# A hand-written order of 1477 steps, reordered behind its first fifth: linear attention followed by a gated long convolution

## The chip, the core and the metric

The kernel runs on one core of one Trainium2 chip. Five engines work beside each other on that core, each with an instruction stream of its own that it executes in order: PE (TensorE, matmuls; its weight loads are listed as PEld), DVE (VectorE), ACT (ScalarE), POOL (GpSimd) and SP (SyncE, which only issues transfers here). Sixteen DMA engines move data. The metric is the device time of one execution in microseconds (us), and the median of several runs is compared.

## The reference, cut to what matters

Two layers follow each other. Eight batches (b = 0 to 7), eight heads, 576 positions, head size 64:

```python
proj = einsum('bhsd,df->bhsf', x, w_phi)                  # x is q, then k; 128 features
proj = proj - max(abs(proj), axis=-1)
phi(x) = concat(exp(proj), exp(-proj))                    # 256 features
kv  = einsum('bhsf,bhsd->bhfd', phi(k), v);  z = sum_s phi(k)
x   = (phi(q) @ kv) / (phi(q) . z + 1e-6)                 # heads side by side: 576 x 512
x1, x2, x3 = split(x @ w_proj)                            # 512 -> 3 * 512
x2  = irfft(rfft(x2) * rfft(filter))                      # along the 576 positions
out = (x1 * x2 * x3) @ w_out
```

The Fourier transforms are matmuls with cosine and sine tables that the kernel makes itself.

## The kernel before, in words

The whole program is a list, `PLAN`, of 1477 words. `run` takes them one after the other; each word names a method of the class `Kernel`, its arguments and, behind an `@`, the first of the eight PSUM banks (0 to 7) in which the step works. The methods issue instructions to their engine at once, so **the order of the words on one engine is the order in which that engine executes**, and nothing reorders it later. Between engines only semaphores hold the order: a step waits until its inputs are there and until the bank or buffer that it writes is free. A word with an engine's name (`Oe,DVE,1,2@7`) says which engine does a step that more than one can do.

Per batch b the words are, in the order of the data:

- `load,n,b` (POOL issues it): q, k or v of a batch from HBM, 576 KB. `trh,n,b,X` (SP): transposes one half by DMA.
- `Pk`, `Qn`, `Pkt`, `Qnt` (PE): projections for the maxima; `maxk`, `maxq` (DVE) reduce them; `mhi`, `mlo`, `trm`, `trme` bring the maxima of q into another layout.
- `ex,k,...` and `ex,q,...` (ACT): the exponentials, of a step of `Pk` or of `Pq`; `exkt`, `exqt` for the remainders. `em,g,b,X` (ACT) is the factor from the maxima and `vs,g,b,X` (POOL or DVE) multiplies v with it, for g = p and m.
- `KV` (PE, 72 matmuls) with its copy `KVe`; `NE`, `NEt` (PE) for numerator and denominator; `rc`, `xn` (DVE) divide.
- `trx`, `trxt` (SP): transpose x by DMA into `xT`, for `X1` and `X3` (PE, 8 matmuls each); `X1t`, `X3t` (16 small matmuls) are the remainders. `X1e` copies x1, `tm` (DVE) multiplies it with x3.
- `f1`, `f2` (POOL or DVE): sums and differences of `xn` that fold the Fourier transform (tiles `SD` and `xf`); `F` (PE) transforms, `Fe` copies to `XF`, `Xl` copies its ends; `X2` (PE) projects in the frequency domain, `Y1` (DVE) multiplies with the filter, `m3` (POOL or DVE) adds; `I` or `J` (PE) goes back, and `Ie`, `Ip`, `Im`, `ym` or `yj` finish y.
- `O,b,c` (PE) is the last product, `Oe,engine,b,c` copies it from PSUM to the tile `o`, and `st,engine,b,c,i` stores one half of it (64 rows).

What the change and the prediction touch besides the order are the rings. `o` has four buffers; they are given out in the order in which `Oe` steps stand in the list, so the copy of a fifth result waits until both halves of the first are stored. `at` and `turn_of` pick the buffer. `vp` and `vm` have three buffers, `kn`, `qn`, `vn` two. SP's queue holds the transposes and the stores in one order: what is behind waits for what is ahead.

The line numbers of the changed file are higher by three than those of the file before from the end of the list on (its text has three more lines), so that L295, the copy on ACT, is L298 there.

Of the kernel before, what the change touches and what calls it, by code (L numbers as in the profile page):

```python
# [69 lines left out]
ym,POOL,0,1 J,0,3@2 maxk,2,2@6 KVe,ACT,1,1@4 NE,1,3@4 ym,POOL,0,2 ex,k,m,2,2@6 yj,0,3@2 NE,1,2@0  # L70
rc,1,3@4 KV,2,0@2 ex,k,p,2,2@6 rc,1,2@0 xn,1,3@4 f1,POOL,1,0,0 xn,1,2@0 trx,1,3 Pqt,1@6 Qn,2,0@4
exqt,m,1@6 f1,POOL,1,1,0 O,0,3@0 maxq,2,0@4 exqt,p,1@6 trx,1,2 O,0,0@1 KVe,ACT,2,0@2 f2,DVE,1,0,1
Oe,ACT,0,3@0 f1,DVE,1,1,1 Qn,2,3@2 trh,q,3,1 Oe,ACT,0,0@1 Qnt,2@4 f2,DVE,1,1,0 f2,POOL,1,1,1
NEt,1@6 maxq,2,3@2 O,0,1@1 trh,k,3,0 f2,POOL,1,0,0 rct,1@6 O,0,2@0 xnt,1,0@6 Oe,ACT,0,1@1 xnt,1,1@6
maxqt,2@4 Pk,2,3@2 trh,k,3,1 Oe,ACT,0,2@0 F,1,2@6 maxk,2,3@2 F,1,3@4 Fe,ACT,1,2@6 F,1,0@0 trh,q,3,0
Fe,ACT,1,3@4 X1,1,3@6 Fe,DVE,1,0@0 ex,k,m,2,3@2 Qn,2,2@4 st,SP,0,1,0 X1e,DVE,1,3@6 em,m,2,1 F,1,1@0
vs,POOL,m,2,1 trxt,1 maxq,2,2@4 X1,1,2@7 Fe,ACT,1,1@0 Qn,3,2@0 st,SP,0,1,1 mhi,2 X2,1,2@4
X1e,ACT,1,2@7 maxq,3,2@0 ex,k,p,2,3@2 load,q,4 X3,1,2@5 Y1,1,2@4 mlo,POOL,2 load,q,5 trm,2@2
X2,1,1@3 trme,ACT,2@2 em,p,2,1 tm,1,2@5 vs,POOL,p,2,1 Pq,2,0@1 Y1,1,1@3 Qn,3,0@4 Pq,2,1@6
ex,q,m,2,0@1 X3,1,3@0 maxq,3,0@4 ex,q,p,2,0@1 load,k,4 X1,1,0@3 ex,q,p,2,1@6 tm,1,3@0 Pq,2,2@4  # L80
ex,q,m,2,1@6 Pkt,3@0 X2,1,3@2 maxkt,3@0 X2,1,0@6 exkt,m,3@0 Y1,1,3@2 exkt,p,3@0 X1,1,1@7
ex,q,m,2,2@4 Y1,1,0@6 NE,2,1@0 X1e,ACT,1,1@7 X3,1,0@2 X1e,ACT,1,0@3 rc,2,1@0 m3,POOL,1,0 xn,2,1@0
ex,q,p,2,2@4 NE,2,0@6 tm,1,0@2 X1t,1@3 rc,2,0@6 Pqt,2@4 xn,2,0@6 X1te,ACT,1@3 Pq,2,3@0 exqt,p,2@4
Xl,DVE,1 Pk,3,1@2 f1,POOL,2,0,1 KV,2,1@6 trh,q,4,1 exqt,m,2@4 maxk,3,1@2 ex,q,p,2,3@0 f1,POOL,2,0,0
X2,1,4@4 st,SP,0,0,0 KVe,ACT,2,1@6 ex,q,m,2,3@0 trx,2,0 NE,2,2@6 m3,POOL,1,1 Y1,1,4@4 X3t,1@5
ex,k,p,3,1@2 rc,2,2@6 NEt,2@0 xn,2,2@6 trx,2,1 X3,1,1@4 ex,k,m,3,1@2 tmt,1@5 rct,2@0 f2,POOL,2,0,0
xnt,2,0@0 NE,2,3@6 trx,2,2 xnt,2,1@0 I,1,0@2 rc,2,3@6 f2,POOL,2,0,1 xn,2,3@6 Ie,1,0@2 I,1,1@0
Im,1,0@2 trx,2,3 Ie,1,1@0 J,1,2@6 tm,1,1@4 f1,POOL,2,1,0 Ip,1,1@0 Im,1,1@0 trxt,2 Pk,3,2@4 Ip,1,0@2
Pk,3,0@0 yj,1,2@6 ex,k,p,3,2@4 ym,POOL,1,0 J,1,3@2 st,SP,0,3,0 maxk,3,0@0 ex,k,m,3,2@4 st,SP,0,3,1
X1,2,0@6 ym,POOL,1,1 st,SP,0,0,1 yj,1,3@2 ex,k,p,3,0@0 X3,2,0@7 trh,k,4,1 maxk,3,2@4 load,v,4  # L90
em,m,3,0 ex,k,m,3,0@0 O,1,0@2 X1e,DVE,2,0@6 trh,q,4,0 em,p,3,0 F,2,0@4 f1,DVE,2,1,1 X1,2,2@6
tm,2,0@7 Fe,ACT,2,0@4 f2,POOL,2,1,0 Qn,3,3@4 Pk,3,3@0 f2,POOL,2,1,1 maxq,3,3@4 O,1,2@7 ex,k,m,3,3@0
X1,2,1@3 vs,POOL,m,3,0 Oe,ACT,1,0@2 Oe,DVE,1,2@7 X1e,ACT,2,2@6 F,2,3@4 maxk,3,3@0 F,2,2@6
st,SP,0,2,1 Fe,ACT,2,3@4 O,1,3@2 X1e,DVE,2,1@3 st,SP,1,0,0 ex,k,p,3,3@0 vs,POOL,p,3,0 Fe,DVE,2,2@6
F,2,1@4 yt,ACT,1 Qn,3,1@0 Fe,ACT,2,1@4 Qnt,3@6 X3,2,2@3 maxq,3,1@0 Oe,ACT,1,3@2 em,p,3,1 O,1,4@4
st,SP,1,3,0 vs,POOL,p,3,1 maxqt,3@6 st,SP,1,2,0 X2,2,2@2 tm,2,2@3 mhi,3 Xl,ACT,2 st,SP,0,2,0
mlo,DVE,3 em,m,3,1 st,SP,1,0,1 Qnt,4@6 Qn,4,0@0 X2,2,0@3 load,k,5 trh,k,4,0 maxqt,4@6 Y1,2,2@2
vs,POOL,m,3,1 X3,2,1@5 Oe,ACT,1,4@4 st,SP,1,2,1 O,1,1@6 Y1,2,0@3 st,SP,1,3,1 trm,3@4 X2,2,3@2
Oe,ACT,1,1@6 maxq,4,0@0 trme,ACT,3@4 X1t,2@3 Pq,3,1@6 tm,2,1@5 X1te,ACT,2@3 KV,3,0@0 Y1,2,3@2
ex,q,m,3,1@6 Pq,3,2@4 ex,q,p,3,1@6 KVe,DVE,3,0@0 m3,POOL,2,1 Pq,3,0@2 X2,2,1@0 ex,q,m,3,0@2  # L100
NE,3,1@6 trh,k,5,0 ex,q,p,3,0@2 Y1,2,1@0 X1,2,3@1 ex,q,p,3,2@4 NE,3,0@2 rc,3,1@6 m3,POOL,2,0
xn,3,1@6 X3,2,3@0 ex,q,m,3,2@4 rc,3,0@2 trx,3,1 xn,3,0@2 Qn,4,2@6 X1e,ACT,2,3@1 Pq,3,3@4 maxq,4,2@6
KV,3,1@2 f1,POOL,3,0,0 st,SP,1,1,1 ex,q,p,3,3@4 st,SP,1,4,0 tm,2,3@0 Pkt,4@6 ex,q,m,3,3@4
f1,POOL,3,0,1 trx,3,0 X2,2,4@1 maxkt,4@6 KVe,ACT,3,1@2 Pqt,3@4 f2,POOL,3,0,1 Y1,2,4@1 exkt,m,4@6
trh,k,5,1 NE,3,3@2 exkt,p,4@6 NE,3,2@0 rc,3,3@2 exqt,p,3@4 xn,3,3@2 I,2,1@6 exqt,m,3@4 rc,3,2@0
Ie,2,1@6 trx,3,3 xn,3,2@0 Pk,4,1@2 X3t,2@4 ex,k,p,4,1@2 Ip,2,1@6 f1,POOL,3,1,1 I,2,2@0 tmt,2@4
trx,3,2 Im,2,1@6 Ie,2,2@0 I,2,0@4 ex,k,m,4,1@2 Im,2,2@0 ym,POOL,2,1 Ip,2,2@0 Pk,4,0@6 trh,q,5,1
Ie,2,0@4 J,2,3@0 maxk,4,1@2 ex,k,p,4,0@6 ym,POOL,2,2 ex,k,m,4,0@6 trh,q,5,0 Ip,2,0@4 X1,3,2@2
Im,2,0@4 yj,2,3@0 ym,POOL,2,0 X1,3,0@3 X1e,ACT,3,2@2 st,SP,1,4,1 maxk,4,0@6 Pk,4,3@0 f2,POOL,3,0,0
Qn,4,1@4 O,2,1@2 maxk,4,3@0 em,p,4,0 X1e,ACT,3,0@3 f1,POOL,3,1,0 O,2,0@6 maxq,4,1@4 ex,k,m,4,3@0  # L110
O,2,3@3 f2,POOL,3,1,1 ex,k,p,4,3@0 Oe,DVE,2,0@6 NEt,3@4 Oe,DVE,2,1@2 load,k,6 st,SP,2,0,1
Oe,ACT,2,3@3 Pk,4,2@6 Qn,4,3@0 rct,3@4 em,m,4,0 ex,k,p,4,2@6 X1,3,1@2 xnt,3,0@4 f2,POOL,3,1,0
xnt,3,1@4 maxq,4,3@0 F,3,0@4 trxt,3 ex,k,m,4,2@6 vs,POOL,p,4,0 X3,3,0@3 Fe,ACT,3,0@4 maxk,4,2@6
st,SP,2,3,0 F,3,2@0 mhi,4 X1e,ACT,3,1@2 F,3,3@4 st,SP,1,1,0 Fe,ACT,3,2@0 vs,DVE,m,4,0 F,3,1@6
mlo,POOL,4 Fe,ACT,3,3@4 Qn,5,2@0 em,p,4,1 X1,3,3@2 Fe,ACT,3,1@6 maxq,5,2@0 Xl,ACT,3 X2,3,2@6
X1e,ACT,3,3@2 tm,3,0@3 em,m,4,1 trm,4@0 X2,3,3@1 vs,POOL,m,4,1 trme,ACT,4@0 Y1,3,2@6 Pq,4,1@2
Qn,5,3@4 Y1,3,3@1 trh,k,6,0 Pq,4,0@6 X3,3,1@0 ex,q,p,4,0@6 maxq,5,3@4 m3,POOL,3,1 st,SP,2,0,0
X2,3,0@1 ex,q,m,4,0@6 st,SP,2,1,1 tm,3,1@0 X2,3,1@4 ex,q,p,4,1@2 Y1,3,0@1 load,q,7 KV,4,0@6
ex,q,m,4,1@2 Y1,3,1@4 vs,POOL,p,4,1 Pq,4,2@0 KVe,ACT,4,0@6 Pq,4,3@2 ex,q,m,4,2@0 NE,4,0@6 X3,3,3@4
ex,q,p,4,3@2 rc,4,0@6 load,v,6 xn,4,0@6 O,2,2@5 ex,q,p,4,2@0 m3,POOL,3,0 tm,3,3@4 trx,4,0 NE,4,1@6  # L120
ex,q,m,4,3@2 KV,4,1@0 rc,4,1@6 xn,4,1@6 Oe,ACT,2,2@5 f1,DVE,4,0,0 Qn,5,0@2 trx,4,1 f1,POOL,4,0,1
Pk,5,0@6 KVe,ACT,4,1@0 maxq,5,0@2 X2,3,4@5 ex,k,m,5,0@6 NE,4,2@0 f2,POOL,4,0,0 ex,k,p,5,0@6
Y1,3,4@5 NE,4,3@2 X3,3,2@4 rc,4,3@2 xn,4,3@2 X1t,3@5 rc,4,2@0 trx,4,3 I,3,1@2 xn,4,2@0 X1te,ACT,3@5
# [991 lines left out]
```

## Time and profile before

| what | value |
|---|---|
| median of three runs | 310.7 us (308.33 to 312.73) |
| profiled execution, from its first to its last instruction | 311.6 us |
| PE busy | 281.0 us, 90% |
| DVE busy | 268.6 us, 86% |
| ACT busy | 216.3 us, 69% |
| POOL busy | 203.8 us, 65% |
| moved by DMA | 40.20 MB, 129 GB/s in the mean |
| granted PE clock, mean | 0.974 |

The profiled execution tells no time of its own beside its span; the span is 0.9 us above the median of the three runs and inside their range. A row of the timeline gives the start, the time taken, the engine, the line, the operation with output and inputs, and in brackets how long the engine had been idle before and what ended that. The list of waits gives who waited for whom: us in total, number of times, longest. A row for DMA issues ends with the median from issue to landing. The prediction quotes the rows that it uses.

### The profile page before, as it was taken

How to read it: one execution, taken by the hardware profiler on the slowest of the kernel's cores; microseconds unless marked ns; L12 is line 12 of the kernel's file. 1: busy time of each engine (PE TensorE's matmuls, PEld its weight loads, DVE VectorE, ACT ScalarE, POOL GpSimd, SP SyncE). 2: the span in 40 equal slices, each digit the busy share in tenths (PEclk: the TensorE clock that was granted, in tenths of full speed). 3: DMA queues.
4: the chain of work that ended last, by engine and by line, in shares of the span. 5: the costliest groups of instructions: out<-in, count | busy, mean ns of one | idle time of the engine just before them, and what ended most of it. 6: DMA issues, size and time to landing. Idle time of an engine off the chain costs nothing.

```text
span 311.6 us, 10240 instructions
## 1 busy us (share of the span) xinstructions
PE 281.0 (90%) x4331; PEld 205.3 (66%) x4360; DVE 268.6 (86%) x447; ACT 216.3 (69%) x345; POOL 203.8 (65%) x163
## 2 busy tenths in 40 slices
...
GB/s 162 235 203 159 136 202 193 105 190 133 91 164 204 94 110 170 116 160 107 114 198 82 131 160 153 172 175 160 84 117 4 56 93 69 19 110 21 1 115 192
DMA packets 72735, 40.20 MB, mean 129 GB/s; under 512 B 53040, under 2 KB 67504, under 8 KB 72688
## 3 DMA queue, kind: packets, MB, share of 16 engines
...
q10 hardware_dynamic: 400, 0.66, 0.8%
q8 instruction: 34, 0.56, 0.8%
...
HBM read 33.75 MB, written 9.44 MB: 139 GB/s over the span
## 4 chain that ended last, share of the span: by engine, by line
PE 70%; DVE 12%; DMA 7%; ACT 5%; issue 3%; SPq 1%; POOL 0%; DVEq 0%; POOLq 0%
PE ps L919 16%; PE ps L897 10%; PE ps L1049 8%; PE ps L764 5%; PE ps L972 4%; PE ps L778 4%; DMA xT<-xn 4%; DMA out_dram<-o 3%; PE ps L1028 3%; PE ps L858 3%; PE ps L862 3%; PE ps L928 2%; DVE mq L707 2%; PE ps L665 2%; PE ps L638 2%
## 5 line engine op out<-in xcount | busy, mean ns | idle before, releaser
L919 PE MATMUL ps<-xT,wproj 128*128 128x256 bf16 x512 | 65.8, 275 | 4.3 <-DVE x1s L960 2.3
L919 PEld LDWEIGHTS <-wproj 128*128 128x128 bf16 x512 | 48.6, 98 | 14.5 <-issue 5.1
L707 DVE TENSOR_REDUCE mk<-ps 128x8 f32<-128x1024 f32 (+1 forms) x40 | 44.0, 1110 | 5.9 <-ACT HTo L295 2.2
L707 DVE TENSOR_REDUCE mq<-ps 128x8 f32<-128x1024 f32 (+1 forms) x40 | 44.0, 1110 | 5.5 <-PE ps L638 4.5
L749 POOL TENSOR_TENSOR vm<-vn,vm 128x1152 bf16<-128x1152 bf16 x14 | 30.4, 2178 | 18.2 <-ACT vm L743 18.2
L749 POOL TENSOR_TENSOR vp<-vn,vp 128x1152 bf16<-128x1152 bf16 x16 | 34.8, 2180 | 10.5 <-ACT vp L743 10.3
L911 POOL TENSOR_TENSOR T<-T,T 128x1024 bf16<-128x1024 bf16 x12 | 25.5, 2124 | 21.9 <-DVE T L907 21.8
L693 ACT ACTIVATE Ekp<-ps 128x1024 bf16<-128x1024 f32 x32 | 32.8, 1030 | 6.6 <-DVE mk L707 3.3
L1038 POOL TENSOR_TENSOR yT<-cv,x1s 128x576 bf16<-128x576 f32 x19 | 24.3, 1289 | 18.3 <-DVE x1s L964 12.8
L852 POOL TENSOR_TENSOR xf<-SD 128x512 bf16<-128x512 bf16 x27 | 31.2, 1170 | 6.7 <-DVE SD L846 5.3
L693 ACT ACTIVATE Ekm<-ps 128x1024 bf16<-128x1024 f32 x32 | 32.8, 1033 | 3.6 <-DVE mk L707 2.7
L693 ACT ACTIVATE Eqm<-ps 128x1024 bf16<-128x1024 f32 x32 | 32.9, 1034 | 3.1 <-PE ps L671 2.9
L1049 PE MATMUL ps<-wout,yT 128*128 128x512 bf16 x133 | 34.3, 385 | 0.7 <-issue 0.2
L693 ACT ACTIVATE Eqp<-ps 128x1024 bf16<-128x1024 f32 x32 | 32.5, 1031 | 3.4 <-PE ps L671 3.3
L846 POOL TENSOR_TENSOR SD<-xn 128x512 bf16<-128x512 bf16 x23 | 26.5, 1160 | 12.6 <-DVE xn L797 12.6
L897 PE MATMUL ps<-wproj,XF 128*128 128x512 bf16 x117 | 30.3, 380 | 0.7 <-issue 0.2
L295 ACT CAST x1s<-ps 128x512 bf16<-128x512 f32 (+1 forms) x30 | 16.0, 548 | 13.1 <-PE ps L928 8.4
L797 DVE TENSOR_TENSOR xn<-ps,r 128x512 bf16<-128x512 f32 x32 | 22.0, 689 | 1.1
L1049 PEld LDWEIGHTS <-yT 128*128 128x128 bf16 x144 | 13.4, 99 | 14.1 <-issue 0.6
L990 ACT COPY es<-ps 128x288 f32<-128x288 f32 x21 | 8.5, 404 | 20.3 <-PE ps L972 19.8
L960 DVE TENSOR_TENSOR x1s<-ps,x1s 128x512 bf16<-128x512 f32 x32 | 21.7, 683 | 0.6 <-ACT x1s L295 0.4
L778 PE MATMUL ps<-KVs,Eqp 128*128 128x65 bf16 x256 | 19.6, 192 | 2.2 <-DVE mq L707 0.6
...
## 6 DMA issues: line engine op xcount, KB each, us to landing
out_dram<-o SPq DMA_DIRECT2D x67, 128.0 KB, 2.9
vn<-in_v_dram POOLq DMA_DIRECT2D x8, 576.0 KB, 7.5
kn<-in_k_dram POOLq DMA_DIRECT2D x7, 576.0 KB, 9.7
qn<-in_q_dram POOLq DMA_DIRECT2D x7, 576.0 KB, 6.6
...
fl<-in_moe_filter_fft_dram SPq DMA_DIRECT2D x8, 128.0 KB, 5.8
out_dram<-o ACTq DMA_DIRECT2D x5, 128.0 KB, 2.8
...
```

What stands on the lines that cost most here:

```text
L693: self.nc.scalar.activation(e, p, AF.Exp, bias=0.0, scale=1.0 if g == "p" else -1.0)
L707: self.nc.vector.tensor_reduce(out=out, in_=src, axis=AX.X, op=ALU.max, apply_absolute_value=True)
L749: self.eng(eng).tensor_tensor(out=t[:, :, :, 0:64], in0=self.at("vn", b)[:, 2 * X:2 * X + 2], in1=t[:, :, :, 64:65].to_broadcast([128, 2, ...
L778: self.mm(self.pb(u, 65 * a, 65 * a + 65), E, KVs[:, u, v, s, :], start=(s == 0), stop=(s == 1))
L797: self.nc.vector.tensor_tensor(out=o, in0=n[:, :, :, 0:64], in1=self.at("r", 4 * b + v).to_broadcast([128, 2, 4, 64]), op=ALU.mult)
L846: self.eng(eng).tensor_tensor(out=o[:, :, 2 * i:2 * i + 2, :], in0=x[:, :, 0:2, :], in1=x[:, :, 2:4, :], op=ALU.subtract if i else ALU.add)
L852: self.eng(eng).tensor_tensor(out=o[:, :, 2 * i:2 * i + 2, :], in0=x[:, :, 0:4:2, :], in1=x[:, :, 1:4:2, :], op=ALU.subtract if i else ALU ...
L897: self.mm(self.pb(0), l, w[:, kt, 512:1024], start=(kt == 0), stop=(kt == 3))
L911: self.eng(eng).tensor_tensor(out=Y, in0=Y, in1=self.at(f"T{2 * e + 1}", b), op=ALU.add)
L919: self.mm(o[:, d], w[:, kt, f0 + 128 * m:f0 + 128 * m + 128], y[:, 1, ::-1, ::-1] if d else y[:, 0], start=(kt == 0), stop=(kt == 3))
L1038: self.eng(eng).tensor_tensor(out=self.at("yT", b)[:, m, 0:SEQ], in0=self.turn_of("cv", (b, m)).rearrange("p x h t -> p (x h t)"), in1=sel ...
L1049: self.mm(self.pb(0), y[:, kt, 128 * c:128 * c + 128], w[:, kt, :], start=(kt == 0), stop=(kt == 3))
```

## The change

The list keeps its first 307 words (21 per cent). Behind these the same 1170 steps stand in another order, with three kinds of difference. Steps move by up to 77 places. In 63 steps that more than one engine can do, the engine is another: for example six `X1e`, five `f1`, four `Oe` and three `Fe` go from DVE to the other engine that can do them, and five `X1e`, four `f1`, four `f2`, four `ym`, three `KVe` and three `Xl` come to DVE. And 239 steps work in another PSUM bank. The order on SP (transposes and stores) is the same word for word, and so is the order of the loads among themselves; where a load stands among POOL's other work is not. No method is changed.

A piece of the list, the words in which the two first differ (`em,p,2,0`, the factor for v, now stands ahead of `Pq,1,2`):

```diff
-m3,POOL,0,0 exkt,p,2@2 Qn,2,1@0 X1e,ACT,0,1@5 tm,0,2@7 Pq,1,0@2 Pq,1,2@4 maxq,2,1@0 ex,q,m,1,0@2
+m3,POOL,0,0 exkt,p,2@2 Qn,2,1@0 X1e,ACT,0,1@5 tm,0,2@7 Pq,1,0@2 em,p,2,0 Pq,1,2@4 maxq,2,1@0
```

Three places follow, all around the end of batch 1 and the middle of batch 2 and 3 (about 112 to 131 us in the trace of before).

**DVE, copies between the steps of batch 2.** Before (`o_1123` is the second buffer of the ring `o`, written here by `Oe,DVE,1,2`; `mk_86` and `mq_88` are maxima of batch 3; `XF_138` is `Fe`):

```order
L960 TENSOR_TENSOR x1s_140<-ps,x1s_140 128x2x8x32
L707 TENSOR_REDUCE mq_88<-ps 128x2x4
L297 COPY o_1123<-ps 128x512
L707 TENSOR_REDUCE mk_86<-ps 128x2x4
L297 CAST x1s_140<-ps 128x2x8x32
L297 CAST XF_138<-ps 128x576
L707 TENSOR_REDUCE mq_88<-ps 128x2x4
```

The same place in the changed kernel:

```order
L963 TENSOR_TENSOR x1s_140<-ps,x1s_140 128x2x8x32
L710 TENSOR_REDUCE mq_88<-ps 128x2x4
L710 TENSOR_REDUCE mk_86<-ps 128x2x4
L300 COPY yT_1120<-yT_1121 128x4x64
L710 TENSOR_REDUCE mq_88<-ps 128x2x2
L710 TENSOR_REDUCE mq_88<-ps 128x2x4
```

The copy to `o`, and the two casts that stood behind it, have left DVE; they are on ACT now.

**ACT, the same stretch.** Before (`vp0_104` is `em,p,3,0`, `Ekm3` and `Ekp3` the exponentials of `Pk,3,3`, `o0_1122` `Oe,1,0`, `o2_1124` `Oe,1,3`):

```order
L743 ACTIVATE vp0_104<-mk1_86 128x18
L295 CAST XF0_138<-ps_61 128x576
L693 ACTIVATE Ekm3_110<-ps_61 128x1024
L295 COPY o0_1122<-ps_61 128x512
L295 CAST x1s0_140<-ps_61 128x2x8x32
L295 CAST XF0_138<-ps_61 128x576
L693 ACTIVATE Ekp3_96<-ps_61 128x1024
L295 COPY yT0_1120<-yT1_1121 128x4x64
L295 CAST XF0_138<-ps_61 128x576
L295 COPY o2_1124<-ps_61 128x512
```

In the changed kernel, where `vp1_105` is `em,p,3,0` and `o1_1123` is `Oe,1,3`:

```order
L696 ACTIVATE Ekp3_96<-ps_61 128x1024
L746 ACTIVATE vm0_118<-mk1_86 128x18
L696 ACTIVATE Ekm3_110<-ps_61 128x1024
L298 CAST x1s0_140<-ps_61 128x2x8x32
L298 CAST XF0_138<-ps_61 128x576
L746 ACTIVATE vp0_104<-mk1_86 128x18
L298 CAST XF0_138<-ps_61 128x576
L746 ACTIVATE vp1_105<-mk1_86 128x18
L298 CAST XF0_138<-ps_61 128x576
L298 COPY o1_1123<-ps_61 128x512
L730 CAST mh1_90<-mq1_88 128x2x18
L298 COPY o2_1124<-ps_61 128x512
```

Both copies to `o` stand behind all casts of `F` here, and the factor for `vs,POOL,p,3,0` has moved from ahead of the first cast to between the second and the third.

**POOL, the loads and the products with v.** Before (`kn_78` is `load,k,5`; `vm_118`, `vp_104`, `vp_105` and `vm_119` are `vs` of m,3,0, p,3,0, p,3,1 and m,3,1):

```order
L590 DMA vn_79<-in_v_dram 128x4x576
L852 TENSOR_TENSOR xf_137<-SD_136 128x2x256 x2
L749 TENSOR_TENSOR vm_118<-vn_80,vm_118 128x18x64
L749 TENSOR_TENSOR vp_104<-vn_80,vp_104 128x18x64
L749 TENSOR_TENSOR vp_105<-vn_80,vp_105 128x18x64
L590 DMA kn_78<-in_k_dram 128x4x576
L749 TENSOR_TENSOR vm_119<-vn_80,vm_119 128x18x64
```

In the changed kernel, where `vp_105` is p,3,0 and `vp_104` p,3,1:

```order
L855 TENSOR_TENSOR xf_137<-SD_136 128x2x256
L593 DMA vn_79<-in_v_dram 128x4x576
L752 TENSOR_TENSOR vm_118<-vn_80,vm_118 128x18x64
L752 TENSOR_TENSOR vp_105<-vn_80,vp_105 128x18x64
L593 DMA kn_78<-in_k_dram 128x4x576
L752 TENSOR_TENSOR vm_119<-vn_80,vm_119 128x18x64
L752 TENSOR_TENSOR vp_104<-vn_80,vp_104 128x18x64
```

The load of k for batch 5 has one product with v less ahead of it.

More of the change, by code (lines that the diff above doesn't have):

```diff
@@ L70 @@
[L70 to L123, printed above, removed]
@@ new lines @@
+ex,q,m,2,0@1 X3,1,3@0 X1,1,0@3 ex,q,m,2,1@6 ex,q,p,2,1@6 st,SP,0,1,1 maxq,3,0@4 Pq,2,2@4 tm,1,3@0
+Pkt,3@0 maxkt,3@0 X2,1,3@2 X2,1,0@6 X1,1,1@7 Y1,1,3@2 Y1,1,0@6 exkt,p,3@0 exkt,m,3@0 NE,2,1@0
+X1e,ACT,1,0@3 X3,1,0@2 ex,q,m,2,2@4 X1t,1@3 rc,2,1@0 load,q,4 ex,q,p,2,2@4 X1e,DVE,1,1@7 xn,2,1@0
+tm,1,0@2 NE,2,0@6 Pq,2,3@0 vs,POOL,m,2,1 load,q,5 vs,POOL,p,2,1 rc,2,0@6 Pqt,2@4 X1te,ACT,1@3
+exqt,p,2@4 xn,2,0@6 load,k,4 exqt,m,2@4 Pk,3,1@2 ex,q,m,2,3@0 KV,2,1@6 maxk,3,1@2 ex,q,p,2,3@0
+X2,1,4@5 trh,q,4,1 ex,k,m,3,1@2 KVe,DVE,2,1@6 f1,DVE,2,0,0 m3,POOL,1,1 NE,2,2@6 NEt,2@0
```

219 lines of the change are left out of this document (135 added, 84 removed).

## The prediction

> **What bounds the kernel now.** I read the busy shares first, then busy time by stretches, PE's list of waits, and the timelines of the four engines around the longest wait.
>
> ```profile
> span 311.6 us, 10240 instructions
> PE 281.0 (90%) x4331; PEld 205.3 (66%) x4360; DVE 268.6 (86%) x447; ACT 216.3 (69%) x345; POOL 203.8 (65%) x163
> 65.00:300.00 235.00, 225.80 (x3587) 170.16 (x3610) 207.41 (x321) 163.49 (x261) 157.72 (x113) 0.99 0.70 115
> 118.50:132.32 13.82, 11.16 (x95) 6.67 (x96) 10.26 (x13) 5.53 (x12) 7.84 (x5) 0.88 0.76 139
> ```
>
> The lower two rows are stretches: their length, busy time and count of PE, PEld, DVE, ACT and POOL, then the granted clock of PE, the DMA share and GB/s. PE is the bound. The kept words reach to about 65 us, and what follows 300 us is the end of the last batch. Between them PE is busy for 225.80 of 235.00 us: 9.2 us of idle time is all that an order of the same matmuls can win there, apart from the clock. DVE is busy for 207.41 and idle for 27.6. The list of PE's waits behind 60 us says where the 9.2 lie (total, count, longest):
>
> ```profile
> PE ps L858 <- DVE o L297: 2.4, 1, 2.4
> PE ps L928 <- issue: 1.6, 1, 1.6
> PE ps L919 <- DMA xT<-xn: 1.1, 1, 1.1
> PE ps L778 <- DVE mq L707: 0.6, 1, 0.6
> PE ps L778 <- DVE xn L797: 0.5, 1, 0.5
> ```
>
> These five make 6.2; the rest are pieces of 0.5 and less. I go through the five, then through what is added.
>
> **Term 1, the wait of 2.4 us for `o`.** Before, PE's `F,2,2` and DVE's copy `Oe,DVE,1,2`, the chain of waits, the loads and products on POOL, and the median landing times of stores, first from 222 to 232 us, where no load is in flight, then from 127.9 to 138.4:
>
> ```profile
> 121.20 0.28 PE L858 MATMUL ps<-Dt,xnt 128*128 128x288 bf16 x1 [2.38 <-DVE o L297]
> 120.46 0.69 DVE L297 COPY o<-ps 128x512 f32<-128x512 f32 x1 [2.99 <-DMA out_dram<-o]
> 121.06 1.21 DVE L707 TENSOR_REDUCE mk<-ps 128x8 f32<-128x1024 f32 x1
> 113.32 7.04 DMA out_dram<-o
> 112.66 0.80 POOL L590 DMA_DIRECT2D vn<-in_v_dram  x1
> 122.31 1.02 ACT L693 ACTIVATE Ekp<-ps 128x1024 bf16<-128x1024 f32 x1 [2.94 <-DVE mk L707]
> 125.85 2.15 POOL L749 TENSOR_TENSOR vp<-vn,vp 128x1152 bf16<-128x1152 bf16 x1 [4.57 <-ACT vp L743]
> 127.94 0.80 POOL L590 DMA_DIRECT2D kn<-in_k_dram  x1
> out_dram<-o SPq DMA_DIRECT2D x7, 128.0 KB, 2.4
> kn<-in_k_dram POOLq DMA_DIRECT2D x1, 576.0 KB, 6.8
> out_dram<-o SPq DMA_DIRECT2D x3, 128.0 KB, 6.3
> ```
>
> A store alone lands after 2.4 us. The store `st,SP,0,0,1` was issued at 113.32, 0.66 us behind `load,v,4` (112.66), and took 7.04, about as long as the load itself. DVE stood 2.99 us until that store had freed its buffer. Behind the copy were queued the maxima of k (121.06) and the cast of `F,2,2`, and PE's bank with them.
>
> After the change no copy to `o` is on DVE here. The buffer goes to `Oe,ACT,1,3`, behind the third cast, and by then the store has landed: this wait goes. It was also dear behind its end, since the granted clock from 118.50 to 132.32 is 0.88 against 0.99 in the large stretch: 11.16 x (1 - 0.88/0.99) = 1.2 us of slower matmuls. So 2.4 + 1.2 = 3.6 is at stake.
>
> What is late next? Follow the new order by durations from the rows. Without the stall, the maxima of k end at about 118.7 (DVE's work before the stall ended at 120.46 - 2.99 = 117.47, and the reduce takes 1.21). The exponential behind them and the casts of `x1` and of `F,2,2` on ACT take 1.02 and twice about 0.6 (the copy of 0.59 quoted below has their shape or nearly), one after the other, and `em,p,3,0`, formerly ahead of all casts, ends at about 121.1. Then `vs,POOL,p,3,0` (2.15, as the product at 125.85) ends at 123.3, and `load,k,5`, which has one product less ahead of it, is issued at 123.3 instead of 127.94. On ACT the last cast, `Oe,1,3` and `Oe,1,2` follow until 123.5. SP's queue holds a store of each of the two, and only then `st,SP,0,2,0`, which was issued at 126.76, ahead of the load, and is now issued at about 124.1: 0.8 us behind the load. That is the position of the 7.04 us store. If it holds as that one, it lands with the load at 123.3 + 6.8 = 130.1. `Oe,ACT,1,4` needs that buffer, as it did before, and reads bank 6, which the new order gives to `Pq,3,1` next:
>
> ```profile
> 129.20 0.59 ACT L295 COPY o<-ps 128x512 f32<-128x512 f32 x1 [1.34 <-issue]
> 129.10 1.04 PE L919 MATMUL ps<-xT,wproj 128*128 128x256 bf16 x8
> 129.97 1.03 PE L1049 MATMUL ps<-wout,yT 128*128 128x512 bf16 x4
> 131.76 0.63 PE L928 MATMUL ps<-xTt,wproj 128*128 128x64 bf16 x16
> 132.32 0.28 PE L665 MATMUL ps<-qT,wphi 64*128 64x256 bf16 x2
> ```
>
> Then `Oe,1,4` ends at 130.7 and `Pq,3,1` starts there, instead of at 132.32. But the new order puts `X3,2,1` (0.87 from start to start) and `X1t,2` (0.56) behind it, so 130.89 would be even: the gain is **0.2**. If the store lands alone, at 126.5, PE doesn't meet it and the gain is **3.6**. I take 0.2, since the one store issued at such a distance behind a load took 7.04, and the three from 127.9 on 6.3.
>
> The Trainium skill ("DMA: Bandwidth & Descriptors", Queues, rings and completion order) says that each DMA engine goes round the queues that have work and changes over after a packet, so that a store would not wait for a load of another queue to finish. By it the store would land early and this term would be the 3.6; the trace disagrees with it in the 7.04 us row, and I keep it as a rival.
>
> **Term 2, 1.1 us before `X1,3,2`.**
>
> ```profile
> 149.33 1.25 PE L919 MATMUL ps<-xT,wproj 128*128 128x256 bf16 x10 [1.08 <-DMA xT<-xn]
> 145.49 2.54 SPq L816 DMA_TRANSPOSE xT<-xn  x2
> xT<-xn SPq DMA_TRANSPOSE x2, 2.5
> ```
>
> The transposes are issued behind `xn` and behind SP's earlier work. `Qn,4,1` (8 small matmuls, 0.3 us) moves ahead of the step as filler, and everything before it shifts by the gain of term 1, consumer and producer alike. Bounds: 0 and 1.08; I take **0.5**.
>
> **Term 3, a gap inside a step.** PE stops amid `X1t,3`, between matmuls with the same inputs and the same bank:
>
> ```profile
> 176.46 0.34 PE L928 MATMUL ps<-xTt,wproj 128*128 128x64 bf16 x6
> 178.38 0.47 PE L928 MATMUL ps<-xTt,wproj 128*128 128x64 bf16 x10 [1.58 <-issue]
> q8 instruction: 34, 0.56, 0.8%
> ```
>
> No datum is missing there, and the page lists a queue that brings instructions; I read the gap as a late fetch while loads fill the engines. In a new order the same place in the stream falls in another step, with other transfers beside it: it can vanish (1.58), stay, or be worse. I take half, **0.8**.
>
> The Trainium skill ("Runtime: NRT & Kernel Launch", Instruction fetch mechanics) says that an engine's stream is refilled in blocks of 256 instructions by a queue of its own and that the cost of a boundary is mostly hidden. By it the gap would be no fetch and go whole with the order that made it, 0.8 more; the 1.58 us between two alike matmuls speaks against "hidden".
>
> **Term 4, DVE beside POOL.** `NE` steps wait for DVE twice, 0.6 and 0.5. In both places a fold on DVE runs beside one on POOL:
>
> ```profile
> 114.24 0.41 DVE L846 TENSOR_TENSOR SD<-xn 128x512 bf16<-128x512 bf16 x1
> 172.41 1.48 DVE L846 TENSOR_TENSOR SD<-xn 128x512 bf16<-128x512 bf16 x1
> 208.28 1.41 DVE L846 TENSOR_TENSOR SD<-xn 128x512 bf16<-128x512 bf16 x1
> 208.25 1.16 POOL L846 TENSOR_TENSOR SD<-xn 128x512 bf16<-128x512 bf16 x1 [0.51 <-DVE xn L797]
> ```
>
> Alone it takes 0.41, beside POOL's 1.41. At 208 us the new order has neither fold between the divisions of batch 5: I book the 0.5 whole. At 172 us the fold is gone too, but an `Oe` and an `m3` have come to DVE ahead of the same maxima: 0 to 0.6, I take 0.3. Together **0.8**.
>
> **Term 5, what is added.** DVE gets four `f2` and three `KVe` more than it had before, and gives away copies of similar size:
>
> ```profile
> L852 DVE TENSOR_TENSOR xf<-SD 128x512 bf16<-128x512 bf16 x5 | 4.3, 854 | 0.1
> L297 DVE CAST KVs<-ps 128x520 bf16<-128x520 f32 x6 | 4.2, 694 | 0.7 <-PE ps L764 0.7
> ```
>
> If every one stood on the path, 4 x 0.854 + 3 x 0.694 = 5.5 us; below nothing it can hardly go, as the copies given away are counted in terms 1 and 4. DVE's 27.6 idle us in the stretch cover it, and if that cover is gone at a place, `NE` waits for the copy. New short waits of a kind not seen before must still be expected among 1170 moved steps: **0.5 lost**, one such copy. The 239 bank changes add no instruction; where a bank is freed later, it is a piece of this term.
>
> **The sum**, against the profiled execution's 311.6, which is 0.9 above the median: -0.2 - 0.5 - 0.8 - 0.8 + 0.5 = -1.8, so 309.8 in such a profile and **308.9** for the median of 310.7.
>
> **The rivals.**
>
> *The store lands alone* (A). The 0.8 us behind the load is only 0.14 more than the distance of the one quoted store, and my 124.1 and 123.3 are each a chain of six durations. If the store is issued ahead of the load, or is served between its packets, term 1 is -3.6: 308.9 - 3.4 = **305.5**. Against it: the 7.04 and the 6.3.
>
> *Nearly all idle time goes* (B): all of the 9.2 is won, 310.7 - 9.2 = **301.5**. For it: the steps that wait in the list all have other neighbours now. Against it: the load moved up in term 1.
>
> *`load,k,6` holds back a transpose* (C, slower). Before, POOL waits for `yj` and issues this load late:
>
> ```profile
> 148.63 1.27 POOL L1038 TENSOR_TENSOR yT<-cv,x1s 128x576 bf16<-128x576 f32 x1 [0.31 <-DVE cv L993]
> 153.29 0.80 POOL L590 DMA_DIRECT2D kn<-in_k_dram  x1
> kT<-kn SPq DMA_TRANSPOSE x2, 6.1
> ```
>
> Now it stands directly behind the `ym` of 148.63, ahead of two `f2` and an `f1`, so some 3 to 4 us earlier. The transposes for `X1,3,2` are issued from 145.49 to 148.03. If the load's issue falls ahead of the second by 0.6 us or more, that transpose takes 6.1 instead of 2.5 and PE stands 3.6 us longer: with nothing won in term 2, 308.9 + 0.5 + 3.6 = **313.0**, and up to 315 with a lowered clock behind it. By before's times the `ym` comes two microseconds too late for that; a transpose as much later decides.
>
> *Nothing is won* (D): the gaps come back at other places, as in term 1, in all terms: **310.7**.
>
> **How the numbers follow.** Forecast 0.42, A 0.26, B 0.07, C 0.12, D 0.13. A measurement of this kernel tells about 2% (6.2 us) from no change. Faster, below 304.5: B whole, nearly half of A (305.5, with the open 1.1 of terms 2 and 4 and 0.8 of term 3 below it), and 0.02 of the forecast: 0.21. Slower, above 316.9: C with a second transpose held, and an added copy on the path in several places: 0.09. The range takes in the forecast, A, D and C's own value, leaving out B and the tail of C: 302 to 314. The forecast's own range, by its terms' bounds, is 306 to 312.
>
> **What would show it.** Term 1: PE's first row of waits is gone, and a copy to `o` on ACT at about 126 to 130 us has waited for the store (forecast) or not (A); the store lands about 6 or 2.4 us after its issue. Term 2: the row `X1` behind `xT` below 1.1. Term 3: no gap "issue" over 1 us inside a step. Term 4: folds on DVE of about 0.4. Rival C: transposes of `xT` with 6 us in the stretch behind 145 us. PE's busy time in the stretch should stay at 226, with less idle. The prediction is wrong if a wait of over 2 us stands at a place that I haven't named.

## The result: slower by 4.6 per cent

The changed kernel took 324.34 us in the median (323.87 to 328.97), the kernel before 309.62 us beside it (308.33 to 312.73). The ratio is 1.0457, with a 95% interval of 1.0367 to 1.0548. Forecast were 308.9 us and a range of 302 to 314. Ratios and their intervals here and below leave out runs over 1.5 per cent above the fastest of their kernel (here the one of 328.97), so that they can differ from the ratio of two medians.

Page and list of waits (PE, from 60 us on) of the changed kernel, and PE, PEld, DVE, ACT and POOL in the stretch from 65 to 300 us:

```profile
span 322.1 us, 10234 instructions
PE 281.1 (87%) x4331; PEld 205.4 (64%) x4360; DVE 279.4 (87%) x452; ACT 216.5 (67%) x345; POOL 201.2 (62%) x158
65.00:300.00 235.00, 216.47 (x3504) 163.47 (x3527) 207.14 (x307) 159.23 (x253) 152.64 (x107) 0.99 0.65 112
PE ps L668 <- ACT o L298: 5.9, 1, 5.9
PE ps L922 <- DVE T L910: 2.4, 1, 2.4
PE ps L861 <- DVE xnt L812: 1.4, 1, 1.4
PE ps L975 <- DVE x1s L963: 1.3, 1, 1.3
PE ps L975 <- DVE xn L800: 0.9, 2, 0.4
```

PE's work is the same, 281.1 us against 281.0. In the stretch it was busy for 216.47 us, 9.3 less than the 225.80 before, so it waited that much longer. All five first waits of the kernel before are gone from the list, and new ones have come: one of 5.9 us for a copy to `o` on ACT, and a row of waits for DVE, whose busy time has grown by 10.8 us (279.4 against 268.6).

Where along the program the time was lost can be read by adding up PE's steps in the order of each list, each at its kind's usual time from start to start, and asking when the two profiles reach the same sum:

```
time in the changed kernel, step     later than before by
 80.8  Pk,2,3                         0.5
121.7  O,1,2                         -3.4   (before's wait of 2.4 has gone)
133.6  Pq,3,1                         2.7   (the wait of 5.9)
138.2  X2,2,1                         4.7   (slow matmuls behind it)
154.3  Pk,4,3                         4.0
161.6  F,3,0                          5.5   (wait of 1.4)
177.1  X3,3,3                         8.1   (wait of 2.4)
186.5  I,3,2                          7.3
224.9  F,5,0                          9.8   (waits of 1.3 and 0.8)
the end                              10.5
```

**The first loss, at the place of the prediction's term 1.** In order: POOL, the chain of waits, the DMA issues between 122.9 and 124.9 us, ACT and PE, and the stretch from 126.0 to 139.1.

```profile
123.09 0.80 POOL L593 DMA_DIRECT2D kn<-in_k_dram  x1
124.21 8.55 DMA out_dram<-o
kn<-in_k_dram POOLq DMA_DIRECT2D x1, 576.0 KB, 9.7
out_dram<-o SPq DMA_DIRECT2D x4, 128.0 KB, 7.2
132.92 1.07 ACT L298 COPY o<-ps 128x512 f32<-128x512 f32 x2 [8.10 <-DMA out_dram<-o]
133.56 0.40 PE L668 MATMUL ps<-qT,wphi 64*128 64x256 bf16 x2 [5.91 <-ACT o L298]
126.00:139.10 13.10, 7.14 (x120) 5.33 (x120) 3.56 (x4) 3.80 (x5) 4.79 (x3) 0.74 0.80 140
```

`load,k,5` was issued at 123.09 and `st,SP,0,2,0` at 124.21, 1.1 us behind it. The store took 8.55 us; the load itself, with the stores and a transpose beside it, took 9.7. ACT stood 8.10 us for the buffer and PE 5.91. The granted clock in the stretch around that wait is 0.74 against 0.99: 7.14 x (1 - 0.74/0.99) = 1.8 us of slower matmuls besides. (The mean hides what the clock does: within that stretch it is 0.50 from 131.4 to 138.0 us.)

**The other losses, on DVE.** Three steps on DVE that read and write SBUF alone, and what POOL did at those times:

```profile
158.76 2.37 DVE L855 TENSOR_TENSOR xf<-SD 128x512 bf16<-128x512 bf16 x1
172.53 3.37 DVE L300 COPY XL<-XF 128x512 bf16<-128x512 bf16 x1
219.38 3.19 DVE L849 TENSOR_TENSOR SD<-xn 128x512 bf16<-128x512 bf16 x1
...
158.49 2.36 POOL L752 TENSOR_TENSOR vp<-vn,vp 128x1152 bf16<-128x1152 bf16 x1
172.05 0.80 POOL L593 DMA_DIRECT2D qn<-in_q_dram  x1
172.84 0.75 POOL L593 DMA_DIRECT2D vn<-in_v_dram  x1
173.60 2.14 POOL L914 TENSOR_TENSOR T<-T,T 128x1024 bf16<-128x1024 bf16 x1
```

The first is `f2,DVE,3,1,1`, the second `Xl,DVE,3`, the third `f1,DVE,5,1,1`; before, ACT did the second and POOL the two others. Each ends 0.2 to 0.3 us behind a piece of POOL's work: 161.13 beside 160.85, 175.90 beside 175.74, and the third 222.57 beside 222.27 (there POOL had a load issue from 219.18, then two folds of 1.17 and 1.15). The copy waits through the end of one load issue, a second one and a product in a row. Groups of DVE by form, before and then after:

```profile
L297 DVE COPY XL<-XF 128x512 bf16<-128x512 bf16 x3 | 0.8, 282 | 0.0
...
L300 DVE COPY XL<-XF 128x512 bf16<-128x512 bf16 x4 | 6.2, 1558 | 0.2 <-ACT XF L298 0.2
L855 DVE TENSOR_TENSOR xf<-SD 128x512 bf16<-128x512 bf16 x8 | 8.2, 1037 | 0.1
```

The same copy takes 282 ns in the mean before and 1558 after.

### The profile page after: what moved, and what is told of

Same layout as the page of the kernel before. It is cut to its first block, busy times and chain, and to the rows that moved or that the text cites. A ratio compares the mean times of both kernels' runs of the same rounds, so it can differ in the third digit from the quotient of the medians.

```text
span 322.1 us, 10234 instructions
## 1 busy us (share of the span) xinstructions
PE 281.1 (87%) x4331; PEld 205.4 (64%) x4360; DVE 279.4 (87%) x452; ACT 216.5 (67%) x345; POOL 201.2 (62%) x158
## 4 chain that ended last, share of the span: by engine, by line
PE 57%; DVE 26%; DMA 5%; ACT 5%; issue 5%; ACTq 1%; POOL 0%; SPq 0%; DVEq 0%; POOLq 0%
PE ps L922 13%; PE ps L1052 7%; PE ps L900 7%; PE ps L767 4%; DVE mq L710 4%; DVE mk L710 4%; PE ps L975 3%; PE ps L781 3%; DVE T L910 3%; DMA xT<-xn 3%; PE ps L1031 3%; DMA out_dram<-o 3%; PE ps L861 2%; PE ps L865 2%; DVE cv L996 2%
## 5 line engine op out<-in xcount | busy, mean ns | idle before, releaser
L849 POOL TENSOR_TENSOR SD<-xn 128x512 bf16<-128x512 bf16 x24 | 28.1, 1182 | 35.2 <-DVE xn L800 35.1
L914 POOL TENSOR_TENSOR T<-T,T 128x1024 bf16<-128x1024 bf16 x13 | 27.5, 2122 | 15.0 <-DVE T L910 14.8
L1041 POOL TENSOR_TENSOR yT<-cv,x1s 128x576 bf16<-128x576 f32 x17 | 22.1, 1309 | 13.2 <-DVE cv L996 12.9
L855 POOL TENSOR_TENSOR xf<-SD 128x512 bf16<-128x512 bf16 x24 | 27.4, 1153 | 3.9 <-DVE SD L849 2.0
L298 ACT COPY o<-ps 128x512 f32<-128x512 f32 x21 | 12.2, 592 | 21.3 <-DMA out_dram<-o 11.3
L298 ACT CAST XF<-ps 128x576 bf16<-128x576 f32 x27 | 16.8, 648 | 11.4 <-PE ps L865 11.2
L298 ACT CAST x1s<-ps 128x512 bf16<-128x512 f32 (+1 forms) x30 | 16.7, 556 | 11.4 <-PE ps L922 4.7
L668 PE MATMUL ps<-qT,wphi 64*128 64x256 bf16 x128 | 16.6, 284 | 6.6 <-ACT o L298 5.9
```

What stands on the lines that cost most here:

```text
L298: self.nc.scalar.copy(dst, src)
L849: self.eng(eng).tensor_tensor(out=o[:, :, 2 * i:2 * i + 2, :], in0=x[:, :, 0:2, :], in1=x[:, :, 2:4, :], op=ALU.subtract if i else ALU.add)
L855: self.eng(eng).tensor_tensor(out=o[:, :, 2 * i:2 * i + 2, :], in0=x[:, :, 0:4:2, :], in1=x[:, :, 1:4:2, :], op=ALU.subtract if i else ALU ...
L914: self.eng(eng).tensor_tensor(out=Y, in0=Y, in1=self.at(f"T{2 * e + 1}", b), op=ALU.add)
L1041: self.eng(eng).tensor_tensor(out=self.at("yT", b)[:, m, 0:SEQ], in0=self.turn_of("cv", (b, m)).rearrange("p x h t -> p (x h t)"), in1=sel ...
```

## The experiments

The runs below were made in groups, and in these the kernel before has medians of 308.7 to 313.5 us. So each ratio is against the runs of before in the same group, and where one profile answers the question, PE's row for 65 to 300 us stands beside it.

### The held stores: four runs

Two of the edits change the place of the stores on SP:

```diff
 st,SP,0,2,1 st,SP,1,0,0
+st,SP,0,2,0 st,SP,1,0,1
 st,SP,1,3,0 st,SP,1,2,0
-st,SP,0,2,0 st,SP,1,0,1
 trh,k,4,0
```

> The changed kernel with the stores st,SP,0,2,0 and st,SP,1,0,1 moved ahead on SP, directly behind st,SP,1,0,0; nothing else. Their data lie ready since about 116 us, so they are issued at about 121.6 and 122.2 instead of 124.21 and 124.85, ahead of load,k,5 (123.1). Theory 'held stores': both land after 2.3 to 2.5 us, the copy to o on ACT no longer waits 8.1 us, PE's wait of 5.9 us before Pq,3,1 goes and with it about 2.0 us of matmuls at a lowered clock: 324.3 - 7.9 = 316.4 us (315 to 318). Rival 'the new order itself is late' (the copy or the bank comes late for another reason): the wait stays or moves to the next step of PE, 322 us or more.

Measured: 316.15 us (315.31 to 317.40), 1.034 of before (1.025 to 1.043): 8.2 below the changed kernel. There is no wait for `o` left. ACT copies as soon as the product is there, and PE goes on at 126.14:

```profile
125.38 0.59 ACT L298 COPY o<-ps 128x512 f32<-128x512 f32 x1 [2.01 <-PE ps L1052]
126.14 0.28 PE L668 MATMUL ps<-qT,wphi 64*128 64x256 bf16 x2
65.00:300.00 235.00, 223.93 (x3534) 167.01 (x3553) 210.81 (x318) 160.34 (x255) 153.53 (x107) 0.99 0.65 113
```

So the wait belongs to the place of the stores. Two things were not as expected. The stores were issued earlier still, at 117.04 and 117.68, and took 6.45 and 6.04 us, not 2.3 to 2.5: `load,v,4` (issued at 111.90) and two transposes were in flight there. They landed at 123.5 and 123.7, just in time. And the wait of 2.4 us before `X3,3,3` is gone too, though nothing was changed on DVE: `Xl,DVE,3` now begins 0.20 us into POOL's first load issue instead of 0.48, and is through in its own time, ahead of the same row of POOL's work.

```profile
163.01 0.28 DVE L300 COPY XL<-XF 128x512 bf16<-128x512 bf16 x1
162.81 0.80 POOL L593 DMA_DIRECT2D qn<-in_q_dram  x1
```

In its place stands a gap of 2.2 us ("issue", L931), of which more below. By this profile the two words are worth 7.5 of the 9.3 us of PE's work that the change lost in the stretch; by the ratios, whose kernel before ran shorter in this group, they take the loss from 4.6 to 3.4 per cent.

With only one store moved (the first of the two `+` words):

> As the run before, but only st,SP,0,2,0 is moved ahead; st,SP,1,0,1 stays and is issued behind load,k,5. Theory 'held stores': Oe,ACT,1,4 is free and Pq,3,1 starts at about 127.5 instead of 133.56, but the next copy, Oe,ACT,1,1, needs the buffer of st,SP,1,0,1, which still lands with the load at about 133; PE then waits at Pq,3,2 (bank 4), for about 4 us, and the time falls by 1 to 3 us only (321 to 323). Rival 'one store is the cause': as with both, 316.4.

Measured: 319.11 us in one run, between the two theories' times. The wait moved to the next copy and the next product, as the first theory has it, but it was shorter than expected, 2.28 us instead of 4: the load started and landed earlier here (122.54 and 130.37). `Xl,DVE,3` took 0.28 us here too, and the gap was 1.9.

```profile
130.46 0.59 ACT L298 COPY o<-ps 128x512 f32<-128x512 f32 x1 [3.59 <-DMA out_dram<-o]
131.09 0.28 PE L668 MATMUL ps<-qT,wphi 64*128 64x256 bf16 x2 [2.28 <-ACT o L298]
```

The opposite edit, on POOL: `load,k,5` one product later.

```diff
-KV,3,0@0 Pq,3,2@4 load,k,5 Y1,2,3@3
+KV,3,0@0 Pq,3,2@4 Y1,2,3@3
-NE,3,0@2 st,SP,1,2,1 vs,POOL,m,3,1 xn,3,1@6
+NE,3,0@2 st,SP,1,2,1 vs,POOL,m,3,1 load,k,5 xn,3,1@6
```

> The changed kernel with load,k,5 moved behind the next product on POOL, vs,POOL,m,3,1, so that it is issued at about 126.5 instead of 123.09; the stores keep their places on SP. Theory 'held stores': the four stores of 123.07 to 124.85 are issued ahead of the load and land after 2.3 to 2.8 us; the wait of 5.9 us at Pq,3,1 goes, the load lands at about 133.4, when it did before; 316.4 us (315 to 318). Rival 'the new order itself': 322 or more.

Measured: 324.14 us (319.52 to 325.86), 1.051 (1.022 to 1.080). The time is the rival's, but not for its reason: the four stores landed after 2.2 to 2.5 us as 'held stores' has it, the wait at `Pq,3,1` was gone, PE was 8.0 us ahead of the changed kernel behind the place, and all of it was given back later. Four rows show the first losses (the DMA issues from 126 to 129 us, then the timelines of SP and PE):

```profile
kn<-in_k_dram POOLq DMA_DIRECT2D x1, 576.0 KB, 8.8
135.48 1.29 SPq L605 DMA_TRANSPOSE kT<-kn  x1
147.78 1.37 PE L922 MATMUL ps<-xT,wproj 128*128 128x256 bf16 x6 [1.57 <-DMA xT<-xn]
157.72 1.03 PE L922 MATMUL ps<-xT,wproj 128*128 128x256 bf16 x8 [1.17 <-ACT o L298]
```

The load was issued at 126.65 and took 8.8 us. `trh,k,5,0` on SP waits for it until 135.48, and the transposes of `xT` and the stores of batch 1 are queued behind. PE paid 1.57 us for the one and 1.17 for the other, both new; with a wait of 0.8 and a lowered clock behind them it had given back 4.3 us by 167 us. Most of the rest went in two further stretches of 3.4 us at a granted clock of 0.50, from 175.2 and from 223.0. Neither of the two places of the load that were tried is good: early it holds the stores, late it holds SP's queue. What helped was the order of SP, which the change had left alone.

### DVE held by POOL: two runs

```diff
-Xl,DVE,3
+Xl,ACT,3
-f2,DVE,3,1,1
+f2,POOL,3,1,1
-f1,DVE,5,1,1
+f1,POOL,5,1,1
```

> The changed kernel with three steps given back to the engines that had them before: Xl,3 to ACT, f2,3,1,1 and f1,5,1,1 to POOL; the order stays. On DVE they took 3.37, 2.37 and 3.19 us beside work of POOL. Theory 'DVE is held by POOL' (both operands in SBUF): DVE gains about 8.9 us, and PE's waits behind them (1.5 before F,3,0, 2.6 before X3,3,3, 1.7 and 0.8 before I,4,2 and F,5,0) go for the larger part: 324.3 - 5 = 319.3 us (317.5 to 321). Rival 'DVE just has too much work': the three take 0.3, 0.4 and 0.4 us of DVE's time by themselves, 323 us.

Measured: 321.86 us (316.56 to 324.30), 1.040 (1.017 to 1.062). The time alone can't separate the theories: it spreads over 8 us. The profile does. PE's work in the stretch rose from 216.47 to 221.72 us, and the waits behind the three steps (1.4, 2.4, 1.3 and the 0.8 before `F,5,0`) are gone from the list, though the gap is back with 1.4:

```profile
65.00:300.00 235.00, 221.72 (x3523) 166.44 (x3541) 204.42 (x313) 160.10 (x254) 155.57 (x109) 0.99 0.67 112
```

The other test leaves DVE its work and changes only when it does it: `Xl,DVE,3` behind `xn,4,0@6`, three DVE steps later, where POOL was idle.

> The changed kernel with Xl,DVE,3 moved behind xn,4,0 on the same engine, where POOL stood idle in the changed kernel's profile (175.74 to 180.64 us); DVE has the same work as before. Theory 'DVE is held by POOL': the step takes about 0.3 us instead of 3.37, the multiplication behind it starts 3.1 us earlier and PE's wait of 2.4 us before X3,3,3 goes. Rival 'DVE just has too much work': its time is the same wherever it stands; the wait stays or moves to the next NE step.

Measured: 322.71 us in one run. The same copy on the same engine:

```profile
174.48 0.28 DVE L300 COPY XL<-XF 128x512 bf16<-128x512 bf16 x1
PE ps L931 <- issue: 1.8, 1, 1.8
```

0.28 us instead of 3.37, and the wait of 2.4 us before `X3,3,3` is gone. So it is POOL's work that held it, not the amount of DVE's; the runs with one and two stores moved say the same, with DVE's list as it was. In its place a gap of 1.8 us "issue" has come back (L931), which the changed kernel's list did not have; that is the gap of the prediction's term 3. In the new order it falls inside `X3t,3`, which stands right ahead of `X1t,3` there (the expectations name the latter).

### Both, and what is left

> The changed kernel with both repairs: the stores st,SP,0,2,0 and st,SP,1,0,1 ahead of load,k,5, and Xl,3, f2,3,1,1 and f1,5,1,1 back on ACT and POOL. If the two causes are separate, their gains add: 7.9 + 5.6 = 13.5 us below the changed kernel, 324.3 - 13.5 = 310.8, less at most 2 us that a gap inside X1t,3 gives back; so 309 to 313, level with the kernel before. Rival 'the new order has a further fault of its own': 315 or more.

Measured: 313.31 us (310.10 to 315.43), 1.0134 of before (1.0059 to 1.0209). That is 2.5 us above what the sum of the two gains gives and just outside what was expected. The two gains are not separate: the wait of 2.4 us for `Xl` was gone with the stores alone and is counted in both. The gap can't be the difference, since all three runs have it (2.2, 1.4 and 1.8); but it is the longest wait that is left. These are its rows, 14 of the 32 matmuls of `X3t,3` and `X1t,3` and then the others, and the loads ahead of it:

```profile
170.56 0.57 PE L931 MATMUL ps<-xTt,wproj 128*128 128x64 bf16 x14
172.94 0.70 PE L931 MATMUL ps<-xTt,wproj 128*128 128x64 bf16 x18 [1.81 <-issue]
162.17 0.81 POOL L593 DMA_DIRECT2D qn<-in_q_dram  x1
162.96 0.75 POOL L593 DMA_DIRECT2D vn<-in_v_dram  x1
```

The second load was moved away from the first:

```diff
-load,q,7 Qn,5,0@3 rc,4,1@6 xn,4,1@6 Pk,5,0@6 load,v,6 m3,DVE,3,0
+load,q,7 Qn,5,0@3 rc,4,1@6 xn,4,1@6 Pk,5,0@6 m3,DVE,3,0
-f1,POOL,4,1,0 Im,3,1@0
+f1,POOL,4,1,0 load,v,6 Im,3,1@0
```

> The kernel with both repairs, and load,v,6 moved from directly behind load,q,7 to behind f1,POOL,4,1,0, about 15 us later. Theory 'a late fetch of instructions behind loads': the gap of 1.8 us amid X1t,3 goes or shrinks below 0.5 us, since no load is in flight there, and nothing needs v of batch 6 before 230 us: 310 us or, against the run with both repairs, 1 to 2 us less. Rival 'the gap belongs to the step': it stays at 1.6 to 2.2.

Measured: 309.15 us in one run, and no gap: the 32 matmuls follow each other in one row, and the second load is issued behind them.

```profile
169.85 1.09 PE L931 MATMUL ps<-xTt,wproj 128*128 128x64 bf16 x32
173.92 0.78 POOL L593 DMA_DIRECT2D vn<-in_v_dram  x1
```

PE's work in the stretch rose from 227.30 to 229.24 us; the one time by itself proves little (the run with both repairs had 310.10 to 315.43). All fourteen profiles together say more. Nine have this gap, of 1.0 to 2.2 us, and in all nine it stands behind the same number of weight loads, 2527, though the step is `X1t,3` in the order of before and `X3t,3` in the new one. Here are the counts of PE and PEld up to the gap, in the kernel before and in the run with both repairs:

```profile
0.00:177.50 177.50, 155.43 (x2509) 112.33 (x2527) 153.47 (x264) 134.75 (x212) 122.16 (x105) 0.96 0.93 151
0.00:172.00 172.00, 150.73 (x2509) 109.48 (x2527) 154.83 (x266) 133.12 (x211) 118.46 (x100) 0.99 0.94 155
```

Of the five without it, three have `load,v,6` moved, and in two (the changed kernel, and `load,k,5` one product later) PE had waited 2.3 to 2.4 us some 6 us earlier. So the gap belongs to a place in PE's stream of instructions and not to a step, and moving the second load, or an earlier wait of PE, takes it away. That fits a late fetch of instructions; that it is the fetch which comes late stays an inference.

Five more steps taken off DVE where POOL held it (`Xl,4` and `Xl,6` to ACT; `m3,0,1`, `f2,1,1,1` and `ym,0,1` to POOL):

> As the run with both repairs, and five further steps that POOL held on DVE by 0.7 to 1.1 us each are given to the other engine: Xl,4 and Xl,6 to ACT, m3,0,1, f2,1,1,1 and ym,0,1 to POOL. Theory 'DVE is held by POOL': DVE gains 4.7 us, PE's part of it is at most the waits that it left (0.8 + 0.7 + 0.3): 0 to 2 us less than with both repairs. Rival 'ACT and POOL are as full': none or 1 us more.

Measured: 310.45 us (307.42 to 313.67), 1.0063 (0.9997 to 1.0128): 2.9 below the run with both, but the intervals overlap. PE's work in the stretch is 228.40 us against 227.30, inside the 0 to 2 us that were expected.

And these with `load,v,6` moved as well:

> The kernel with both repairs and the five further steps off DVE, with load,v,6 moved as in the run beside it. If the gap is a late fetch, 1 to 2 us less than without the move (310.45): 308 to 309.5, level with the kernel before or up to 1% below it. Rival 'the gap belongs to the step': 310.5.

Measured: 309.37 us (306.11 to 313.17), 0.9966 of before (0.9932 to 1.0001). The gap is gone here too; that the time is 1.1 us below the run without the move is within the spread of both. With two stores and one load moved and eight steps given to other engines, the new order is level with the old one and no better.

### The kernel before, by the same three causes

> The kernel before, unchanged, with a second profile: its executions differ by several us, and the profile that the prediction read may be one of the longer ones. If the wait of 2.4 us for o belongs to the order, it is there again, and a difference in time lies in the stretch up to 65 us; rival: it is an accident of that execution and is absent in a shorter one, so that the changed kernel had nothing to win there.

Measured: 312.04 us, span 310.3. The wait for `o` is there again, 1.7 us, and the gap too: 1.2 inside `X1t,3`, and another of 1.3 inside `NE,5,2`, behind 3039 weight loads, 512 further on. So the wait belongs to the order, and the gap to its place in the stream, both with sizes that vary.

One word moved in the kernel before, `load,v,4` from behind `maxk,3,2@4` to behind `f2,POOL,2,1,0`:

> The kernel before with one word moved: load,v,4 stands behind f2,POOL,2,1,0 and is issued at about 115.9 us instead of 112.66, behind the store st,SP,0,0,1 (113.32) instead of 0.66 ahead of it. Theory 'held stores': that store lands in 2.4 us instead of 7.04, the copy to o on DVE starts at about 117.5, PE's wait of 2.4 us goes, with up to 1.2 us of slower matmuls: 1.5 to 3.6 us less than the kernel before. Rival 'the stall comes back at a later transfer' (as when load,k,5 was issued late): no difference.

Measured: 311.32 us (309.72 to 316.59), 1.0092 (1.0019 to 1.0165): no gain. The copy to `o` started at 117.41 and its wait was gone, as expected, but PE stood again at `O,1,1`:

```profile
117.41 0.68 DVE L297 COPY o<-ps 128x512 f32<-128x512 f32 x1
123.35 3.99 DVE L731 TENSOR_TENSOR mh<-mq,mh 128x36 bf16<-128x36 f32 x1
127.99 1.46 PE L1049 MATMUL ps<-wout,yT 128*128 128x512 bf16 x4 [1.99 <-DVE mq L707]
```

`mlo`, a step of 128 x 36, which took 0.63 before, took 3.99 us, as it fell among POOL's products and a load issue; behind that wait the granted clock was 0.50 for 3.4 us. A stall removed had moved DVE's next step beside POOL. So the three causes were put together in the kernel before, with three words:

```diff
-load,v,4                (behind maxk,3,2@4)
+load,v,4                (behind f2,POOL,2,1,0)
-mlo,DVE,3
+mlo,POOL,3
-load,v,6                (behind rc,4,0@6)
+load,v,6                (behind f1,POOL,4,1,0)
```

> The kernel before with three words changed: load,v,4 behind f2,POOL,2,1,0 (as tried alone), mlo,3 on POOL instead of DVE, where it took 3.99 us beside POOL's products when load,v,4 was late and made PE wait 2.0 us, and load,v,6 behind f1,POOL,4,1,0. If held stores, DVE held by POOL and the late fetch are the three causes of before's own waits, the wait of 2.4 us for o, its return at O,1,1 and the gap amid X1t,3 (1.6) all go: 2 to 4 us below the kernel before, about 306 to 307.5. Rival 'each removed wait comes back at the next transfer': no difference, 309 to 310.

Measured: 306.52 us (305.87 to 307.22), 0.9827 of before (0.9772 to 0.9882). It is shorter than the kernel before in its own group, by less than the 2 per cent that the prediction asks of a clear change; of the 52 runs of before in all groups, six are as short (305.52 to 307.01). So it is likely faster, and by how much stays open; the three words were not tried one by one, save the first. Its list of PE's waits has nothing above 0.9 (the gap behind 3039 weight loads), and the step that had taken 3.99 us takes 0.24 on POOL:

```profile
122.92 0.24 POOL L731 TENSOR_TENSOR mh<-mq,mh 128x36 bf16<-128x36 f32 x1
65.00:300.00 235.00, 228.98 (x3604) 171.03 (x3626) 209.52 (x324) 163.74 (x263) 158.36 (x115) 1.00 0.71 119
```

## Why the prediction was wrong

**Term 1** named the place, the two transfers and the wait that would come: load at 123.3 and store at 124.1 were forecast, 123.09 and 124.21 measured; rival A, a store that lands alone, is out. The Trainium skill's rule for it ("DMA: Bandwidth & Descriptors", Queues, rings and completion order: an engine goes round its queues packet by packet) does not save a store here; 8.55 us for the store behind the load stands against 2.4 for one without. What failed is the size. The load was given the 6.8 us of one load of before, and took 9.7, and the store landed with it at about 132.8 instead of 130.1. A range was to be had: the other loads of k behind 90 us took 8.7, 6.5 and 10.4 in the same trace. What made it longer is not shown; three stores were issued in the 2 us behind it, where before there was one transpose, but with three stores it took 7.8 in the run with one store moved, and with one store and a transpose 9.2 in the run with two. The forecast also counted the slow clock behind a stall for the stall that goes (1.2 us) and not for the one that comes (1.8). A gain of 0.2 was forecast; between 81 and 138 us the place cost 4.7 - 0.5 = 4.2.

**Term 5** is the step that failed outright: "0.5 lost, one such copy". The added steps on DVE were priced at their group's mean of before (0.854 and 0.694) and bounded by 5.5 us in all; the three costly ones took 2.37, 3.37 and 3.19 each, and two of them, an `Xl` and an `f1`, were of kinds that the term had not priced at all. The rows for it stood in term 4, 0.41 alone against 1.41 beside POOL, but were used only for the folds that leave DVE. What comes to DVE was not laid beside POOL's new order. So the wait of 2.4 us before `X3,3,3` stood at a place that the prediction had not named. From 154.3 to 224.9 us this made 5.8 us, net of what other waits gave back, and giving back the three steps won 5.3 us of PE's work. With the 4.2 of term 1 this is 10.0 of the 10.5 us between the two profiles.

**Term 3** took 0.8 for the gap. It was absent from the changed kernel, by luck and not by the order: PE stood 2.4 us at `X3,3,3` shortly ahead of it, and in all six runs of the new order without that wait and with `load,v,6` in its place the gap was there again (1.4 to 2.2). So nothing was won. That the same place in the stream falls in another step was right. The Trainium skill ("Runtime: NRT & Kernel Launch", Instruction fetch mechanics) says that the cost of passing from one block of instructions to the next is mostly hidden; if the gap is such a passage, it is not hidden in nine of the fourteen profiles, which show it with 1.0 to 2.2 us.

**Term 2** was right in its direction: the wait of 1.08 us for `xT` went whole, also in the run with both repairs, where PE is not late. **Term 4** was right for the two places that it spoke of, whose waits are gone; what it did not see is that another fold of batch 5, `f1,5,1,1`, comes from POOL to DVE at 219 us, where it was held for 3.19.

**Rival C**, the held transpose, did not happen: `load,k,6` was issued at 154.21, behind the transposes. The slow case came by two mechanisms that were both in the text, and were priced as even (term 1) and as half a microsecond (term 5). The **base** was a little off too: a run's time lies 1.8 us above its span here (322.1 and 323.88), so the profile read was of an execution of some 313.4 us, one of before's longer ones.
